# One run of small matmuls for the values of a pair of tiles and the scores of the next pair

## The chip, the cores and the metric

The kernel runs on one core of a Trainium2 chip (trn2). The metric is the device time of one execution in microseconds (us); lower is better. Engines are named as in the profile: PE (TensorE matmul), PEld (its weight loads), DVE (VectorE), ACT (ScalarE), POOL (GpSimd), SP (SyncE, which issues the DMAs).

## The reference

Three stages in a row, all in float32: chunked attention over 4 batches, 8 heads, 768 positions of width 64, and then two feed-forward layers (512 to 2048 to 512) over the 3072 tokens.

```python
for c in range(nc):                                  # chunks of 32 queries
    k_ctx = k[:, :, max(0, c*32 - 16) : min(S, c*32 + 40)]   # and v_ctx
    k_full = concatenate([mem_k, k_ctx], axis=2)     # 8 memory keys; v_full alike
    scores = q_c @ k_full.T / sqrt(64)
    a = exp(scores - max(scores)); a = a / (sum(a) + 1e-9)
    out[c] = a @ v_full
h = x @ w_in;  y = (max(h, 0) + alpha * min(h, 0)) @ moe_w_out      # layer 1
h = y @ w2_in; out = (h * tanh(softplus(h))) @ moe2_w_out           # layer 2
```

## The kernel before

The 3072 tokens are 24 tiles of 128 tokens and six blocks of four tiles. The attention of a block is computed while the layer 1 of the block before it runs; layer 2 follows after all of layer 1. Matrices of the layers are split into a high and a low part, so each product takes three matmuls.

**Layer 1.** For every block `blk` and every `j` of the 16 slices of the hidden width, `gemm1` (L990) does 12 large matmuls (128 x 512) into one PSUM bank, bank 4 or 5 by `j % 2`. `act1` (L1019) empties that bank with two activations on ACT (L1021, L1022), joins them on DVE (L1025) and splits the result into `gh` on ACT (L1015) and `gl` on DVE (L1016). `gemm2` (L1059, matmuls L1051) does 12 large matmuls into the accumulators in banks 0 to 3. A list `pend` keeps `gemm2` behind: with `LAG = 2` the order on PE is `gemm1(j)`, `gemm2(j-2)`, `gemm1(j+1)`, `gemm2(j-1)`, and so on.

**Attention.** From tile 4 on, tiles are taken in pairs `T`, `T+1`. `scores_late` (L699) does 128 small matmuls (64 rows, 32 columns of the array, 64 moving columns) into banks 6 and 7; then come maxima on DVE, 32 exponentials on ACT with their sums, and the normalisation on DVE. From tile 8 on (`UPT`) `turn_late` (L846) turns the result on DVE with 16 stream transposes (L877) into the one buffer `aT`. `values_late` (L776) does 128 small matmuls (64 rows, 64 columns, 32 moving columns), also into banks 6 and 7, which ACT (L810) and DVE (L813) empty into the `x` of the block. Each of these runs is one task of PE, a `burst` (L891): nothing comes between its matmuls.

**Order.** `block_steps` (L928) lists for every pair the steps `("s", T)`, None, a turn or None, `("v", T)`; `weave(p)` (L1355) spreads the eight steps of two pairs over 30 positions, two to each `j`: one after `gemm1(j)`, one after `gemm2(j-2)`. So a pair's scores and its values are two separate bursts among the large matmuls.

**The plan.** All tasks go into `Plan` (L68): each has an engine, an assumed duration, and what it reads and writes. PE's tasks get their place in the order in which they are added; every other task gets a due time counted back from the PE task that needs it, and each engine takes of its ready tasks the one that is due first. What comes out is a fixed order for each engine; on the chip each engine waits in that order.

**Loads of attention.** SP's queue loads `q` of a tile into `q_own[T % 2]`, and the keys of an even tile into `kring` (one buffer), its values into `vring` (one buffer). An odd tile has one room, `upper`, the upper halves of two buffers: its keys are loaded there (L522), and, when the scores have read them, its values (L559), into the same place.

**Weights of layer 1.** The second matrix has 16 slices in slots `("o", 0)` to `("o", 15)`. After the first block the slices from `AWAY = 10` on give their slots to other uses: each was stored to DRAM once (L1329) and is loaded again in every later block by `reload1` (L396, L400), through three slots in turn. Slots 13 to 15 serve the conversion of the layer 2 weights, which runs on ACT, DVE and SP during blocks 1 to 4.

## Time and profile before

| | |
|---|---|
| time, median of 3 runs | 1084.5 us (1083.97 to 1085.22) |
| the profiled execution: its time | 1084.67 us |
| its span, first to last instruction | 1082.9 us |
| PE busy | 1073.2 us, 99% of the span, 9299 matmuls |
| DVE, ACT busy | 729.5 us (67%), 657.0 us (61%) |
| DMA | 252.63 MB, mean 233 GB/s |

Matmuls overlap in the array, so the busy time of PE is not the sum of what single matmuls cost: that is read from the distance between starts. A row of the timeline merges neighbours of one kind: its start, the time from the start of the first to the end of the last, and the count. Idle time of an engine other than the one that sets the end costs nothing.

### The profile page before, as it was taken

What the parts mean: (1) busy time and instruction counts of PE and PEld (TensorE: products, weight loads), DVE (VectorE), ACT (ScalarE), POOL (GpSimd) and SP (SyncE); (2) the same over time, 40 slices, a digit from 0 to 9 for tenths busy, and PEclk for the clock granted to TensorE, in tenths of its full rate; (3) what the DMA queues carried; (4) which work ended last, traced back from release to release, by engine and by line L of the source; (5) the groups of instructions that cost most, each with busy time, mean ns of one, the idle gap of its engine ahead of it and who ended that gap; (6) DMA issues with size and microseconds to landing.
All of it is one profiled execution on the core that took longest, in us unless ns stands there. A gap on an engine that the chain in (4) does not pass through costs nothing.

```text
span 1082.9 us, 24507 instructions
## 1 busy us (share of the span) xinstructions
PE 1073.2 (99%) x9299; PEld 966.5 (89%) x9299; DVE 729.5 (67%) x1614; ACT 657.0 (61%) x1676; POOL 6.6 (1%) x19
## 2 busy tenths in 40 slices
PE   9999999999999999999999999999999999999997
PEld 6888888878888888888888999999999999999997
DVE  6899487677769768686322855676685676676555
ACT  6888456455464646555334766676676666666664
POOL 2000000000000000000000000000000000000000
PEclk9999999999999999999999999999999999999999
DMA  9957754775476577547764777887887888887875
GB/s 300 321 184 240 249 187 167 243 242 194 166 259 216 176 240 262 184 144 248 228 193 141 253 241 252 267 266 249 271 264 252 272 260 258 264 263 236 263 248 170
DMA packets 139942, 252.63 MB, mean 233 GB/s; under 512 B 13872, under 2 KB 45104, under 8 KB 139824
## 3 DMA queue, kind: packets, MB, share of 16 engines
q1 hardware_dynamic: 139824, 251.07, 72.1%
q8 instruction: 73, 1.20, 0.5%
q14 instruction: 45, 0.37, 0.1%
HBM read 205.92 MB, written 45.09 MB: 232 GB/s over the span
## 4 chain that ended last, share of the span: by engine, by line
PE 98%; DMA 1%; DVE 0%; ACT 0%; SPq 0%; issue 0%; DVEq 0%; ACTq 0%
PE bank L1003 24%; PE bank L1051 24%; PE bank L1183 22%; PE bank L1256 22%; PE bank L789 2%; PE bank L723 1%; PE bank L1313 1%; DMA raw<-in_w_in_dram 1%; PE bank L600 0%; PE bank L667 0%; PE bank L836 0%; SPq L559 0%; DVE rstrip L1277 0%; PE bank L860 0%; DVE e L1277 0%
## 5 line engine op out<-in xcount | busy, mean ns | idle before, releaser
L1003 PE MATMUL bank<-xh,wi 128*128 128x512 f32 (+1 forms) x784 | 254.8, 387 | 0.0
L1051 PE MATMUL bank<-gh,wo 128*128 128x512 f32 x768 | 253.9, 391 | 0.7 <-ACT rstrip L250 0.7
L1003 PEld LDWEIGHTS bank<-xh,wi 128*128 128x128 f32 x784 | 146.3, 188 | 30.0
L1051 PEld LDWEIGHTS bank<-gh,wo 128*128 128x128 f32 x768 | 144.2, 188 | 31.3 <-ACT rstrip L250 1.1
L1191 ACT COPY v<-bank 128x512 f32<-128x512 f32 x192 | 102.5, 534 | 114.4 <-PE bank L1183 111.4
L1003 PE MATMUL bank<-xl,wi 128*128 128x512 f32 (+1 forms) x392 | 150.9, 385 | 0.0
L1051 PE MATMUL bank<-gl,wo 128*128 128x512 f32 x384 | 149.5, 389 | 0.0
L1025 DVE SCALAR_TENSOR_TENSOR rstrip<-rstrip,nalpha 128x512 f32<-128x512 f32 x96 | 71.8, 748 | 70.9 <-ACT rstrip L1022 70.1
L1015 ACT CAST gh<-rstrip 128x512 fp32r<-128x512 f32 x96 | 60.2, 627 | 88.2 <-DVE rstrip L1025 47.9
L1021 ACT ACTIVATE rstrip<-bank 128x512 f32<-128x512 f32 x96 | 58.0, 604 | 87.6 <-PE bank L1003 85.2
L1194 DVE TENSOR_TENSOR v<-v,v 128x256 f32<-128x256 f32 x192 | 80.4, 423 | 44.2 <-ACT v L1191 42.7
L1016 DVE TENSOR_TENSOR gl<-rstrip,gh 128x512 fp32r<-128x512 f32 x96 | 66.3, 691 | 57.2 <-ACT gh L1015 56.8
L1197 ACT ACTIVATE v<-v 128x256 f32<-128x256 f32 x192 | 80.1, 418 | 36.7 <-DVE v L1194 34.2
L1194 DVE TENSOR_TENSOR v<-v 128x256 f32<-128x256 f32 x144 | 60.8, 423 | 51.9 <-ACT v L1191 48.1
L1003 PEld LDWEIGHTS bank<-xl,wi 128*128 128x128 f32 x392 | 73.7, 188 | 14.4
L1051 PEld LDWEIGHTS bank<-gl,wo 128*128 128x128 f32 x384 | 72.1, 188 | 14.6
L1183 PE MATMUL bank<-wo,wi 128*128 128x256 f32 x432 | 61.9, 283 | 0.6 <-ACT v L1191 0.6
L742 ACT ACTIVATE s<-bank,su 128x64 f32<-128x64 f32 x160 | 48.5, 350 | 19.7 <-DVE su L759 19.7
L877 DVE STREAM_TRANSPOSE aT<-s 32x256 f32<-32x256 f32 x128 | 55.7, 435 | 2.9
L1022 ACT ACTIVATE rstrip<-bank 128x512 f32<-128x512 f32 x96 | 57.5, 599 | 0.0
L1183 PEld LDWEIGHTS bank<-wo,wi 128*128 128x128 f32 x432 | 56.3, 192 | 1.1 <-ACT v L1191 1.0
L1183 PE MATMUL bank<-xl,wi 128*128 128x256 f32 x396 | 54.4, 283 | 0.0
(197 smaller groups left out, 1890.1 us busy)
## 6 DMA issues: line engine op xcount, KB each, us to landing
wi<-w2o SPq DMA_DIRECT2D x204, 256.0 KB, 3.5
wo<-w2o SPq DMA_DIRECT2D x132, 256.0 KB, 3.4
wo<-w1o SPq DMA_DIRECT2D x30, 512.0 KB, 4.5
w2o<-wo SPq DMA_DIRECT2D x56, 256.0 KB, 2.4
wi<-w2s SPq DMA_DIRECT2D x56, 256.0 KB, 3.5
wo<-in_w_out_dram SPq DMA_DIRECT2D x24, 512.0 KB, 7.7
w2k<-wo SPq DMA_DIRECT2D x40, 256.0 KB, 2.2
wo<-w2s SPq DMA_DIRECT2D x40, 256.0 KB, 3.3
```

The source lines that it names most:

```text
L1003: nc.tensor.matmul(bk.t[:, lo:hi], a, b, start=kk == 0 and i == 0, stop=kk == KT - 1 and i == 2)
L1015: add("act", a_(n), lambda: nc.scalar.copy(g.t[0], src.t[0]), [src], [(g, "h")])
L1016: add("dve", d_(n), lambda: nc.vector.tensor_sub(g.t[1], src.t[0], g.t[0].bitcast(F32)), [src, (g, "h")], [(g, "l")])
L1021: add("act", a_(n) - 0.05, lambda: nc.scalar.activation(m.t[0], h.t[:, :n], AF.Relu, scale=-1.0), [h], [m])
L1022: add("act", a_(n) - 0.05, lambda: nc.scalar.activation(r.t[0], h.t[:, :n], AF.Relu), [h], [r])
L1025: lambda: nc.vector.scalar_tensor_tensor(r.t[0], m.t[0], nalpha[:, j : j + 1], r.t[0], ALU.mult, ALU.add),
L1051: nc.tensor.matmul(bk.t[:, :n], lt, rh, start=j == 0 and i == 0, stop=j == NJ - 1 and i == 2)
L1183: nc.tensor.matmul(X.t[:, half * HB : (half + 1) * HB], l, r, start=start and kk == n == 0, stop=kk == 1 and n == 2, skip_group_check=True,)
L1191: add("act", c_(n * HB), lambda: nc.scalar.copy(e.t[:, : n * HB], X.t[:, : n * HB]), [X], [(e, i) for i in range(n)])
L1194: add("dve", e_(HB), lambda: op(at(to), at(a), at(b)), [v[a], v[b]], [v[to]])
L1197: add("act", c_(HB), lambda: nc.scalar.activation(at(name), at(name), AF.Mish), [], [v[name]])
L1256: nc.tensor.matmul(bk.t[:, s * HB : (s + 1) * HB], g.t[:, zg * HB + s * P : zg * HB + (s + 1) * P], piece()[:, zw * HB : (zw + 1) * HB], s ...
```

## The change

From tile 8 on, the values of pair `T` and the scores of pair `T+2` become one burst of kind `"vs"`. There are seven of these (`T` = 8 to 20 in steps of two); the scores of pair 8 and the values of pair 22 stay alone, as do both bursts of pairs 4 and 6.

The values of a joint burst go into the two banks of `gemm1`, `4 + (j+1) % 2` and `4 + j % 2`, and the scores into banks 6 and 7, so that it writes four banks. It is put only at an odd position, after `gemm2(j-2)`, and behind it `ahead()` brings the oldest pending `gemm2`, that of `j-1`, forward. The order on PE is then `gemm1(j)`, `gemm2(j-2)`, burst, `gemm2(j-1)`, `gemm1(j+1)`, `gemm1(j+2)`, `gemm2(j)`.

When the burst is issued, the values of an odd tile and the keys of the next odd tile must both be there. So odd tiles get a second room in slot `("o", 12)`, and the two rooms are taken in turn by pairs. `AWAY` falls from 10 to 9: slices 9 to 15 are stored and loaded again, through slots 9 to 11. All loads for the next pair follow the burst.

```diff
@@ -281,7 +281,8 @@
     w2s = dp.tile([P, NPAIR * len(SENT), 512], F32, name="w2s")
     w2o = dp.tile([P, NPAIR * 7, 512], F32, name="w2o")
     w2_bufs = {"k": Buf(None), "s": Buf(None), "o": Buf(None)}
-    AWAY = 10
+    AWAY = 9
+    ROOM = 12
     w1o = dp.tile([P, NJ - AWAY, 1024], F32, name="w1o")
     w1o_buf = Buf(None)
 
@@ -507,6 +508,17 @@
         kts[T], qs[T] = (kt, kview), (qt, qview)
         att_bufs.append(kt)
 
+    rooms = [upper]
+
+    def room(T):
+        return rooms[T // 2 % 2 if T >= UPT else 0]
+
+    def open_room():
+        before = slots["o", ROOM]
+        b = slot("o", ROOM, [P, 1024], F32)
+        rooms.append([Buf(lambda lo=lo: b.t[:, lo : lo + 512], before) for lo in (0, 512)])
+        slots["o", ROOM] = rooms[1]
+
     def load_qk_late(T):
         b, t = divmod(T, TPB)
         qt = q_own[T % 2]
@@ -515,8 +527,8 @@
             lambda: nc.sync.dma_start(qt.t, q[b, t].rearrange("h d a e x -> (h d) (a e x)")), writes=[qt],
         )
         if T % 2:
-            bufs = upper
-            for i, u in enumerate(upper):
+            bufs = room(T)
+            for i, u in enumerate(bufs):
 
                 def part(i=i, u=u):
                     nc.sync.dma_start(
@@ -548,12 +560,12 @@
             att_bufs.append(v)
             return
 
-        bufs = upper if T % 2 else [vring.next()]
+        bufs = room(T) if T % 2 else [vring.next()]
         for e in range(2):
             half = slice(e * 64, (e + 1) * 64)
             rows = vw[b, 2 * t + e].rearrange("w h d -> w (h d)")
             if T % 2:
-                for c, u in enumerate(upper):
+                for c, u in enumerate(bufs):
 
                     def part(c=c, u=u, half=half, rows=rows):
                         nc.sync.dma_start(u.t[half], rows[c * CH : c * CH + SW])
@@ -773,10 +785,10 @@
 
         return go, [b for i in range(2) for b in kts[T + i][0] + qs[T + i][0]], bks, rest
 
-    def values_late(T):
+    def values_late(T, places=(6, 7)):
         ab, aT = aTs.pop(T)
         vs = [vws.pop(T + i) for i in range(2)]
-        bks = [bank(6), bank(7)]
+        bks = [bank(i) for i in places]
 
         def go():
             for i, (_, value) in enumerate(vs):
@@ -891,14 +903,23 @@
     def burst(T, kind, *parts):
 
         add(
-            "pe", 1.15 if T < T0 else {"s": 1.55, "v": 2.1}[kind], lambda: [go() for go, _, _, _ in parts],
-            sum((r for _, r, _, _ in parts), behind(T)), sum((w for _, _, w, _ in parts), []),
+            "pe", 1.15 if T < T0 else {"s": 1.55, "v": 2.1, "vs": 3.35}[kind], lambda: [go() for go, _, _, _ in parts],
+            sum((r for _, r, _, _ in parts), behind(T) if kind != "vs" else []), sum((w for _, _, w, _ in parts), []),
         )
         for *_, rest in parts:
             rest()
 
-    def run_step(st):
+    def run_step(st, free=None):
         kind, T = st
+        if kind == "vs":
+            burst(T, kind, values_late(T, free), scores_late(T + 2))
+            load_v(T + 3)
+            load_v(T + 2)
+            for T2 in (T + 4, T + 5):
+                if T2 < NTT:
+                    load_qk(T2)
+            turn_late(T + 2)
+            return
         if kind == "t":
             (turn_pe if T < T0 else turn_late)(T)
         elif kind == "v":
@@ -912,7 +933,7 @@
             T2 = T + 1 if T < T0 else T + 2
             if T2 < NTT:
                 load_qk(T2)
-                if T < T0:
+                if T < T0 or T >= UPT:
                     load_qk(T2 + 1)
         if kind == "v" and T >= T0 - 1:
             T2 = T + 1 if T < T0 else T + 2
@@ -928,7 +949,10 @@
     for blk in range(1, NBA):
         steps = []
         for T in range(blk * TB, (blk + 1) * TB, 2):
-            steps += [("s", T), None, ("t", T) if T < UPT else None, ("v", T)]
+            if T < UPT:
+                steps += [("s", T), None, ("t", T), ("v", T)]
+            else:
+                steps += [("s", T) if T == UPT else None, None, None, ("vs", T) if T + 2 < NTT else ("v", T)]
         block_steps.append(steps)
 
 
@@ -1341,6 +1365,8 @@
     LAG = 2
     tiles = [(0, blk, j) for blk in range(NBA) for j in range(NJ)]
     pend = []
+    joint = []
+    open_room()
     xcur = xts[0]
     xnext = None
     n_in = 0
@@ -1352,10 +1378,22 @@
         att = block_steps[blk + 1] if layer == 0 and blk + 1 < NBA else []
         p0 = P0 if blk == 0 else 0
 
+        def ahead():
+            done = pend.pop(0)
+            if done[1] and done[2] >= AWAY:
+                reload1(done[2])
+            gemm2(*done)
+
         def weave(p):
             lo, hi = ((len(att) * max(x - p0, 0) + NPOS - p0 - 1) // (NPOS - p0) for x in (p, p + 1))
             for st in filter(None, att[lo:hi]):
-                run_step(st)
+                if st[0] == "vs":
+                    joint.append(st)
+                else:
+                    run_step(st)
+            if joint and p % 2:
+                run_step(joint.pop(), (4 + (j + 1) % 2, 4 + j % 2))
+                ahead()
 
         if j == 0:
             if blk == NBA - 1:
@@ -1373,10 +1411,7 @@
         act1(blk, j, h, n)
         pend.append((layer, blk, j))
         while len(pend) > LAG:
-            done = pend.pop(0)
-            if done[1] and done[2] >= AWAY:
-                reload1(done[2])
-            gemm2(*done)
+            ahead()
         if blk == NBA - 1:
             while n_in < len(in_places) and in_places[n_in][0] <= j:
                 reload_in(n_in)
```

## Rows read from the trace of the kernel before

**Rows 1.** Page: granted clock in 40 slices, and the chain that ended last.

```profile
PEclk9999999999999999999999999999999999999999
...
PE 98%; DMA 1%; DVE 0%; ACT 0%; SPq 0%; issue 0%; DVEq 0%; ACTq 0%
```

**Rows 2.** Waits of PE from 20 us on: line, releaser, us, times, longest.

```profile
PE bank L1051 <- ACT rstrip L250: 0.7, 1, 0.7
PE bank L1183 <- ACT v L1191: 0.6, 1, 0.6
```

**Rows 3.** Instructions of L723 and of L789: count, duration ns, first and last start.

```profile
L723 PE MATMUL bank<-kt,qbd x640: 212/216/243, 37.8 to 451.9; 64*32 64x64 f32 x160
...
L789 PE MATMUL bank<-aT,vw x640: 219/219/241, 64.9 to 483.8; 64*64 64x32 f32 x160
```

**Rows 4.** Chain in order of time: one undisturbed group of 12 large matmuls.

```profile
47.69 2.72 PE bank L1051 x12
```

**Rows 5.** Timeline of PE around the values of pair 8: start, us, line, count.

```profile
152.15 0.39 PE L1051 MATMUL bank<-gh,wo 128*128 128x512 f32 x1
152.47 1.14 PE L789 MATMUL bank<-aT,vw 64*64 64x32 f32 x64
153.42 1.11 PE L789 MATMUL bank<-aT,qbd 64*64 64x32 f32 x64
154.47 0.50 PE L1003 MATMUL bank<-xh,wi 128*128 128x512 f32 x1
...
157.32 0.39 PE L1051 MATMUL bank<-gh,wo 128*128 128x512 f32 x1
```

**Rows 6.** Timeline of PE around the scores of pair 10.

```profile
165.26 0.39 PE L1051 MATMUL bank<-gh,wo 128*128 128x512 f32 x1
165.58 0.86 PE L723 MATMUL bank<-kt,qbd 64*32 64x64 f32 x64
...
166.74 0.34 PE L723 MATMUL bank<-qbd 64*32 64x64 f32 x12
167.02 0.49 PE L1003 MATMUL bank<-xh,wi 128*128 128x512 f32 x1
...
169.88 0.39 PE L1051 MATMUL bank<-gh,wo 128*128 128x512 f32 x1
```

**Rows 7.** Timeline of PE in the first attention: four small runs behind each other.

```profile
13.23 0.92 PE L836 MATMUL bank<-ident,s 64*96 64x64 f32 x16
14.07 1.19 PE L600 MATMUL bank<-wo,wi 128*64 128x64 f32 x32
15.10 1.10 PE L667 MATMUL bank<-aT,vw 96*64 96x64 f32 x32
16.13 0.92 PE L836 MATMUL bank<-ident,wo 64*96 64x64 f32 x16
```

**Rows 8.** Windows: length, busy times of the engines, granted clock, DMA.

```profile
13.20:17.00 3.80, 3.80 (x97) 3.56 (x97) 2.49 (x7) 3.47 (x20) 0.00 (x0) 1.00 1.09 308
```

**Rows 9.** Timeline of PE in the scores of pair 16.

```profile
311.57 0.86 PE L723 MATMUL bank<-kt,qbd 64*32 64x64 f32 x64
...
312.36 0.32 PE L723 MATMUL bank<-qbd,qbd 64*32 64x64 f32 x13
```

**Rows 10.** Timeline of all engines ahead of and behind the values of pair 12.

```profile
245.28 0.39 PE L1003 MATMUL bank<-xh,wi 128*128 128x512 f32 x1
...
247.07 0.62 ACT L1015 CAST gh<-rstrip 128x512 fp32r<-128x512 f32 x1 [5.66 <-DVE rstrip L1025]
...
248.09 0.59 ACT L1022 ACTIVATE rstrip<-bank 128x512 f32<-128x512 f32 x1
248.32 1.02 PEld L789 LDWEIGHTS bank<-aT,vw 64*64 64x64 f32 x64 [0.35 <-issue]
...
251.88 0.69 DVE L813 TENSOR_TENSOR xl<-bank,xh 128x512 fp32r<-128x512 f32 x1
```

**Rows 11.** Reloads of L400: from issue to landing, min/median/max.

```profile
DMA to landing us min/median/max: 3.7/4.5/6.6
```

## The prediction

> **What bounds the kernel now.** I read the page first: the chain that ended last lies to 98% on PE, and the granted clock is full in all 40 slices [rows 1], so the end moves only when PE does less or waits more. The waits of PE come next: from 20 us on there are two, of 0.7 and 0.6 us, and neither is near an attention burst [rows 2]. There is no wait for this change to remove. What is left is time inside PE's own stream, and for that the timeline has to be read by starts, because matmuls overlap (a small one lasts 0.22 us, but its neighbour starts long before that) [rows 3].

> The undisturbed stream is 12 large matmuls in 2.72 us, 0.227 us each [rows 4]. Around the values of pair 8 the stream shows this [rows 5]:

> - In: the last large matmul starts at 152.15, so the next thing could start at 152.377. The first small one starts at 152.47: 0.093 us lost.
> - The run itself: the last of the 128 starts at 153.42 + 1.11 - 0.219 = 154.311 and its pitch is (1.11 - 0.219) / 63 = 0.014, so the run is over at 154.325, after 1.855 us.
> - Out: the next large matmul starts at 154.47: 0.145 us lost. Its group of 12 takes until 157.32, 2.85 us and not 2.72: 0.13 us more.

> The values are a detour of 2.22 us, of which 0.37 us is switching. The scores are the same picture [rows 6]: in 165.58 - 165.487 = 0.093, the run 1.294 us at a pitch of 0.0102, out 167.02 - 166.874 = 0.146, and a first group of 2.86 us, 0.14 over; together 1.67 us. Each line has 640 matmuls of its first half, 64 to a burst, so there are ten bursts of each kind [rows 3].

> **The change part by part.** *The joint burst.* Seven times, the way out of the values (0.145 + 0.13) and the way into the scores (0.093) go: 0.368 us. In their place comes a switch from values (64 x 64 of the array) to scores (64 x 32), which the trace of before does not hold. The nearest rows are the four small runs behind each other in the first attention [rows 7]. With 0.22 us as length of one matmul, L836 has a pitch of 0.70 / 15 = 0.047, is over at 13.977, and L600 starts at 14.07: 0.09 us. L600 (128 x 64) to L667 (96 x 64), in the same way, 15.10 - 15.071 = 0.03. L667 to L836 (64 x 96), 16.13 - 16.008 = 0.12. The two rows in which the columns change cost 0.09 and 0.12, the one in which they stay 0.03. Here the columns change, so I take 0.10; the bounds are 0 (no switch at all) and 0.368 (as dear as the way through the large matmuls). That is 0.268 us a burst, 7 x 0.268 = 1.88 us.

> [...]

> *Length of the burst.* It becomes some 3.5 us of small matmuls. The granted clock stays 1.00 through 3.8 us of small runs with nothing large between them [rows 8], so I cost that at nothing.

> *Banks of the values.* The values now wait for the two activations of `act1(j)` on ACT; the group `gemm2(j-2)`, 2.72 us, hides them where ACT is prompt. Everything on PE is queued behind that wait. The other side: `gemm1(j+1)` needs the first of the two banks back. In the trace the first subtraction behind the values of pair 12 ends at 251.88 + 0.69 = 252.57 [rows 10], 2.25 us after that run (248.32 + 2.00, the length as in [rows 5]); between lie now the scores (1.29), the way out (0.15) and `gemm2(j-1)` (2.86), 4.3 us. Nothing, with 2 us to spare; without that cover, 2.25 us a burst.

> *`ahead`.* `gemm2(j-1)` moves before `gemm1(j+1)`, but behind the burst, so its `g` has more time than before (3.5 us against 2.72). The work on PE is the same.

> *Loads.* After a joint burst SP's queue gets the loads that came in two portions: values of an odd tile 4 x 128 KB, of an even tile 2 x 256 KB, `q` 2 x 256 KB, keys 336 and 2 x 168 KB, 2.2 MB, some 9 us at the mean 233 GB/s. The next joint burst is 15 positions of 2.72 us, 41 us, later: nothing. What stands behind them in the queue are the reloads of layer 1 (35 instead of 30) and the layer 2 conversion. A reload lands in 4.5 us, 6.6 at most [rows 11]; its slot comes free three `gemm2` ahead, 3 x 5.44 less the 2.72 by which `ahead` brings one forward, 13.6 us: hidden; one that is late would cost PE up to 6.6 us. The one store more lies with the six others behind the first block's loads; PE does not wait for it.

> **The sum.** The profiled execution took 1084.67 us, 0.17 above the median of the runs and well within their spread of 1.25. 1084.67 - 1.88 = 1082.8; from the median it would be 1082.6. I predict 1082.7 us. That is 0.17% less, and 0.2% (2.2 us) is about what a measurement of this kernel tells from no change.

> **The rivals.**

> *No drain in the middle, so faster.* For it: 64 rows stay 64 rows, and the row with equal columns cost 0.03 [rows 7]. Against it: here the columns do change. With 0.03 the gain is 7 x 0.338 = 2.37, 1082.3 us; with 0, 1082.1. It passes 0.2% from a switch of 0.058 us down.

> *The joint run is not what it says, so no gain.* Either the middle switch costs all of 0.368, or the longer stream of small matmuls has holes. The scores of pair 16 have one: their second half should start at 311.57 + 64 x 0.0102 = 312.22 and starts at 312.36, and nothing in the profile released it [rows 9]. Against it: of the bursts on which this rests it is one; the pitch of [rows 6] runs through. Two such holes in each joint burst cost 7 x 0.28 = 1.96 us: 1084.7 us.

> *ACT is late for the values' bank, so slower.* ACT works in a fixed order. Ahead of the values of pair 12 it stood 5.66 us for DVE before a cast, with the two activations behind that; `gemm1`'s last matmul had started at 245.28, and the second activation ended at 248.09 + 0.59 = 248.68, 0.36 us after the values started [rows 10]. Before, that was harmless: the values took banks 6 and 7. Now PE would stand some 0.4 us. From 0.27 us a burst the gain is gone, and from (1.88 + 2.17) / 7 = 0.58 the kernel is slower by 0.2%. The worst that row allows: had the matmuls ended when ACT began to stand, the activations would end 5.66 + (248.68 - 247.07) = 7.3 us later, a wait of over 4 us, 7 x 4 = 28 us. With 0.4 in each burst the time is 1085.6, with 1 us, which I take as its middle, 1084.67 - 1.88 + 7 = 1089.8. Against it: the plan now counts these activations due before the values and will take them ahead of exponentials; and a pair has 15 or 16 positions instead of 11 from scores to values, 41 us instead of 30, so DVE's turning is done earlier and does not pile up there.

> **How the numbers follow.** Forecast, a middle switch of 0.06 to 0.12 and at most two or three short waits: 0.45, 1082.4 to 1083.7. No drain: 0.25. No gain: 0.18. ACT late by enough to be slower: 0.12. The range holds the first three, from 1082.1 less the half spread of the runs (0.6), 1081.5, up to the lighter end of the last, 1085.6; I leave out the heavier part of it, some 0.1, and a little below. Faster by over 0.2% is the second case and the lower edge of the forecast (0.07): 0.32. Slower is the last: 0.12. Within 0.2%: 0.56.

> **What would show it.** In the timeline of PE after: nine entries into small matmuls from tile 8 on instead of sixteen; a joint run of 1.86 + 0.10 + 1.29 us, with one group of 2.86 behind it; the gap between last value and first score is the disputed number. Right on ACT: no wait of PE for L1021, L1022, L810 or L813. Wrong would be the prediction if PE's waits name these lines seven times, or if it waits for a reload (L400) or an odd tile's loads (L522, L559).

## The result, and the profile after

The changed kernel takes 1098.42 us (four runs, 1097.1 to 1099.61) against 1084.24 us: ratio 1.0129, 95% interval 1.0117 to 1.014. It is 14.2 us slower, outside the predicted range. The span of the profiled execution grew from 1082.9 to 1096.8 us.

The page of the changed kernel, of which the first line and the chain answer to [rows 1] (L735 is now the line of the scores, L801 of the values, L1027 of `gemm1`, L1075 of `gemm2`):

```profile
span 1096.8 us, 24496 instructions
...
q8 instruction: 73, 1.20, 0.5%
...
PE 98%; issue 1%; DVE 0%; ACT 0%; DVEq 0%; ACTq 0%
```

A share of the chain has grown from 0% to 1%: "issue", time in which PE waited for nothing that the profile names. The waits of PE say where, beside [rows 2]: line, releaser, us, times, longest.

```profile
PE bank L735 <- issue: 11.2, 7, 2.6
...
PE bank L735 <- PE bank L801: 0.5, 1, 0.5
```

Seven times for seven joint runs, in the scores. No line of ACT, DVE or a load (L822, L825, L1045, L534, L571) is among PE's releasers in attention. The timeline of PE in the first joint run, values of pair 8 with scores of pair 10, which answers to [rows 5] and [rows 6]:

```profile
152.16 0.39 PE L1075 MATMUL bank<-gh,wo 128*128 128x512 f32 x1
152.48 1.14 PE L801 MATMUL bank<-aT,vw 64*64 64x32 f32 x64
153.44 1.11 PE L801 MATMUL bank<-aT,qbd 64*64 64x32 f32 x64
154.48 0.80 PE L735 MATMUL bank<-kt,qbd 64*32 64x64 f32 x60
...
156.44 0.83 PE L735 MATMUL bank<-wo,qbd 64*32 64x64 f32 x60 [1.06 <-issue]
157.19 0.50 PE L1075 MATMUL bank<-gh,wo 128*128 128x512 f32 x1
...
160.05 0.39 PE L1027 MATMUL bank<-xh,wi 128*128 128x512 f32 x1
```

The values end at 153.44 + 1.11 - 0.219 + 0.014 = 154.345 and the scores start at 154.48: the disputed switch costs 0.135 us. Then, with 68 of 128 scores issued, PE stands still. What happened meanwhile is in the DMA view of two stretches, 154.1 to 155.2 and 155.2 to 156.5; the first holds one packet, the second none of that queue.

```profile
DMA packets 1, 0.02 MB, mean 15 GB/s; under 512 B 0, under 2 KB 0, under 8 KB 0
...
q8 instruction: 1, 0.02, 5.6%
```

```profile
DMA packets 15, 0.04 MB, mean 31 GB/s; under 512 B 0, under 2 KB 0, under 8 KB 15
...
q1 hardware_dynamic: 15, 0.04, 14.4%
```

Queue q8 carries 73 packets of 16 KB in all. The trace holds 18,834 instructions of PE, which is 73 packets of 256 and a rest of 146; 64 bytes an instruction is my estimate from these two counts. I took the start and length of each packet from the trace and counted where in PE's program (weight loads, matmuls, semaphore waits) the first matmul behind each hole stands, modulo 256 (its place within a block of 256):

```
joint run  hole from, to (us)   place mod 256   last q8 packet, end   from its end to resuming
152.48     155.16  156.44       197             154.12, 155.10        1.33
200.94     202.79  203.55       197             201.06, 202.06        1.49
200.94     204.83  207.11       196             204.66, 205.82        1.30
252.61     255.20  256.82       197             254.23, 255.38        1.44
301.42     304.63  307.41       197             304.98, 305.97        1.44
351.45     353.98  355.43       196             353.00, 353.97        1.46
400.12     403.29  405.59       197             403.19, 404.14        1.45
451.24     453.68  454.65       196             452.41, 453.37        1.28
```

All eight holes lie at one place of a period of 256, wherever that falls in the run, and each ends 1.28 to 1.49 us after a packet of instructions has landed. The one from 202.79 to 203.55, between values and scores, is the wait that the view puts down to L801. (Counted from the records of the trace alone, the places are 193 and 194; what matters is that they agree.) The reading is that PE has run out of instructions; the experiments test it.

A second cost follows in two runs. The timeline of PE behind the run at 200.94:

```profile
207.11 0.21 PE L735 MATMUL bank<-qbd 64*32 64x64 f32 x1 [2.06 <-issue]
207.25 0.50 PE L1075 MATMUL bank<-gh,wo 128*128 128x512 f32 x1
207.59 0.56 PE L1075 MATMUL bank<-gl,wo 128*128 128x512 f32 x1
207.95 1.05 PE L1075 MATMUL bank<-gh,wo 128*128 128x512 f32 x2
...
211.70 0.40 PE L1027 MATMUL bank<-xh,wi 128*128 128x512 f32 x1
```

The large matmuls start 0.43 us apart instead of 0.227, and the group takes 211.70 - 207.25 = 4.45 us instead of 2.86. The windows view of that stretch (length, busy times, granted clock, DMA) shows half the clock, 0.51:

```profile
207.60:211.00 3.40, 3.40 (x10) 2.63 (x9) 3.40 (x7) 0.41 (x1) 0.00 (x0) 0.51 0.09 34
```

**The account.** Measured as in the prediction, from the last large matmul before to the end of the group behind, the first joint run costs 157.19 + 0.14 - 152.387 = 4.94 us; the seven are 4.94, 8.13, 5.29, 6.50, 5.15, 7.59 and 4.68, together 42.3 us. The fourteen runs that they replace cost 27.5. That is 14.8 us, and the span grew by 13.9; the 0.7 us wait of L1051 in [rows 2] is gone. Nearly all of it is the holes: less the ordinary distance between starts, the eight are 13.2 us, and the large matmuls at half clock add 1.6 us and 1.3 us; the switches saved give 1.6 us back.

### The profile page after: what moved, and what is told of

Read it like the earlier page. It is cut to its first block, busy times and chain, and to the rows that moved or that the text cites. A ratio compares the mean times of both kernels' runs of the same rounds, so it can differ in the third digit from the quotient of the medians.

```text
span 1096.8 us, 24496 instructions
## 1 busy us (share of the span) xinstructions
PE 1076.0 (98%) x9299; PEld 969.9 (88%) x9299; DVE 725.6 (66%) x1610; ACT 657.6 (60%) x1680; POOL 6.6 (1%) x19
## 4 chain that ended last, share of the span: by engine, by line
PE 98%; issue 1%; DVE 0%; ACT 0%; DVEq 0%; ACTq 0%
PE bank L1075 24%; PE bank L1027 24%; PE bank L1207 22%; PE bank L1280 22%; PE bank L801 2%; PE bank L735 1%; PE bank L1337 1%; PE bank L612 0%; PE bank L679 0%; PE bank L848 0%; DVE rstrip L1301 0%; PE bank L872 0%; DVE e L1301 0%; ACT L1221 0%; DVEq L1497 0%
## 5 line engine op out<-in xcount | busy, mean ns | idle before, releaser
L1075 PE MATMUL bank<-gh,wo 128*128 128x512 f32 x768 | 256.0, 394 | 0.0
L1027 PE MATMUL bank<-xh,wi 128*128 128x512 f32 (+1 forms) x784 | 252.7, 386 | 0.0
L1075 PEld LDWEIGHTS bank<-gh,wo 128*128 128x128 f32 x768 | 145.6, 190 | 33.3 <-DMA kt<-in_kw_dram 2.5
L1027 PEld LDWEIGHTS bank<-xh,wi 128*128 128x128 f32 x784 | 146.3, 188 | 29.6
L1027 PE MATMUL bank<-xl,wi 128*128 128x512 f32 (+1 forms) x392 | 150.8, 385 | 0.0
L1075 PE MATMUL bank<-gl,wo 128*128 128x512 f32 x384 | 150.6, 392 | 0.0
L1045 ACT ACTIVATE rstrip<-bank 128x512 f32<-128x512 f32 x96 | 58.1, 606 | 92.6 <-PE bank L1027 92.4
L1027 PEld LDWEIGHTS bank<-xl,wi 128*128 128x128 f32 x392 | 73.7, 188 | 14.6
L1075 PEld LDWEIGHTS bank<-gl,wo 128*128 128x128 f32 x384 | 72.8, 190 | 14.8
L371 ACT CAST wo<-wo 128x256 fp32r<-128x256 f32 x64 | 24.1, 406 | 52.3 <-DVE wo L365 47.8
```

What stands on the lines that cost most here:

```text
L1027: nc.tensor.matmul(bk.t[:, lo:hi], a, b, start=kk == 0 and i == 0, stop=kk == KT - 1 and i == 2)
L1045: add("act", a_(n) - 0.05, lambda: nc.scalar.activation(m.t[0], h.t[:, :n], AF.Relu, scale=-1.0), [h], [m])
L1075: nc.tensor.matmul(bk.t[:, :n], lt, rh, start=j == 0 and i == 0, stop=j == NJ - 1 and i == 2)
```

## The experiments

The theory ("supply theory" below): PE's instructions arrive in blocks of 256, and only the next block is ahead. While large matmuls run, 256 instructions take 29 us (128 x 0.227); in a joint run they take 1.3 to 1.9 us, and in the eight cases of the table the next block was there 2.6 to 4.3 us after the one before it had been entered. A run of 128 small matmuls with their weight loads, 256 instructions, gets by (no wait at L723 or L789 in [rows 2]); a joint run, 512, cannot. The rivals: the room, the banks and the loads; or a limit on runs of small matmuls as such.

**Large matmuls between the two parts.** In three kernels all else of the change stays (the edit, shortened):

```diff
-            burst(T, kind, values_late(T, free), scores_late(T + 2))
+            burst(T, "vv", values_late(T, free))
+            between()       # 12, 6 or 3 of the matmuls of gemm2(j-1); the rest follow the scores
+            burst(T, "ss", scores_late(T + 2))
```

> All parts of the change stay (second room, three reload slots from slice 9 on, values in the banks of gemm1, the order of the loads), but gemm2(j-1) stands between the values and the scores, so no run of small matmuls holds more than 128. Supply theory (PE runs out of instructions: they come in blocks of 256, one block ahead, and a joint run of 128 + 128 small matmuls with their weight loads is 512 instructions): no hole in any run, switching as before, 1084.2 us, between 1083.5 and 1085.5. Rival (the room, the banks, the reloads or the order of the loads cost time by themselves): holes or waits stay in or around the scores, 1090 us or more.

> The same with six large matmuls between. Supply theory: 1.6 us and 15 instructions more between the boundaries; no hole in six of the joint runs, 0.3 to 0.8 us twice in the one that begins 4 instructions before a boundary: 1084.3 to 1086 us. Rival (length of the run as such): 1084.3 us.

> The changed kernel with three of the twelve matmuls of gemm2(j-1) between the values and the scores of a joint run, the other nine behind it. Supply theory: from one boundary of 256 instructions to the next there must be some 2.9 to 3.3 us; the three large matmuls and the switch add 0.9 us and 8 instructions to the 1.9 us of before, so holes shrink from 1.1 to 2.8 us to 0 to 0.8 us each, in all 1 to 5 us: 1085 to 1089 us. Rival (a run of small matmuls fails as such, above a length between 128 and 256): no run is longer than 128 now, no hole at all, 1084.3 us.

With twelve: 1083.91 us, ratio 0.9995 (0.9986 to 1.0004), as expected. The room, the banks, the reloads and the order of the loads cost nothing that the time shows. With six 1087.88, with three 1096.04 (one run each; single runs of the kernel before reach 1087.09, so for six the three holes count and not the time). The waits of PE in scores, first with six, then with three:

```profile
PE bank L735 <- issue: 3.4, 3, 1.6
```

```profile
PE bank L735 <- issue: 7.6, 7, 3.3
```

With twelve there is none. All holes are at the block boundary again, and all ten end 1.24 to 1.70 us after a packet. Three large matmuls still leave seven holes though no run is longer than 128, so the length of a run as such is out. Both times are above what I expected, six by 2 and three by 7 us: with six, three runs had holes where I counted on one. Those three came to the second boundary 2.5 to 3.0 us after the first, the other four 3.2 to 3.4 us after it, with a delay of at most 0.13 us. But the block can take longer than the 2.9 to 3.3 us that I counted on: in the run at 392.64 the first boundary is crossed at 394.31, the packet starts only at 396.14, and PE resumes at 399.03, 4.7 us after the crossing. With three, one hole of 3.3 us and 6.8 us at half clock behind it carry much of the excess.

**The values twice, in the kernel before.** The plan's assumed duration of these runs goes from 2.1 to 4.0 us with it.

```diff
-            for i, (_, value) in enumerate(vs):
+            for i, (_, value) in list(enumerate(vs)) * (2 if T >= UPT else 1):
```

> The kernel before, with the values of the pairs from tile 8 on computed twice in the same run (the same results written again), so eight runs of 256 small matmuls, with nothing of the change: no second room, old banks, old loads. The second computation costs 8 x 1.86 = 14.9 us of PE. Supply theory: where both block boundaries fall well inside the run (counted in the program, in five of the eight: after 138, 126, 113, 100 and 247 of its 512 instructions) a hole of 1.2 to 1.6 us at the second boundary, where the first is crossed at the start (30, 17, 4) little or none; in all 5 to 12 us of holes, 1104 to 1111 us, 1106.7 us. Rival (holes come from the new room, banks or loads): no hole, 1099.2 us.

1118.05 us (one run), with nothing of the change in it. Holes: in the five runs expected, and behind two of the others, in the first large matmuls. The waits:

```profile
PE bank L789 <- issue: 7.1, 5, 1.9
PE bank L1051 <- DVE xl L813: 1.8, 1, 1.8
...
PE bank L1051 <- issue: 0.8, 1, 0.8
```

The rival's 1099.2 fails. The time is 7 us above my upper bound. The seven holes are 11.6 us between starts, at the upper end of what I expected; I had not counted that the clock fell to half in four stretches, 17 us in all. The wait of 1.8 us that the view puts down to DVE is the hole behind the run at 406.69: it lies at a block boundary and ends 1.44 us after a packet.

**Moving the boundaries.** Empty instructions (padding of the program to an address, in PE's stream; what they cost, the control below measures) are spread among the large matmuls ahead of each joint run, so that every run begins the same distance before a boundary. The work and its order stay (the edit, shortened):

```diff
             def go(kk=kk, views=views, k0=k0, at=pads_of(blk, j, -1)):
+                if at:      # (8, 0) in 40 to 48 groups of three matmuls ahead of a run,
+                    nc.tensor.addr_align(at[0], offset=at[1])   # (256, offset) in the last one
                 xh, xl = (t[:, kk - k0, lo:hi] for t in views())
```

> The changed kernel, with some 840 empty instructions spread among the large matmuls, so that each of the seven joint runs begins 14 instructions before a boundary of 256. Nothing else differs. Supply theory: the first boundary is crossed ahead of the run, while the sequencer still runs ahead of large matmuls, the second has its block by then, the third comes some 7 large matmuls after the run: holes of 0 to 0.4 us a run instead of 1.1 to 2.8, and 7 x 0.23 = 1.6 us of saved switching: 1082.6 us, between 1082 and 1086. Rival (data, banks, or the length of the run of small matmuls as such): holes as in the changed kernel, 1097 to 1100 us.

> The same with each joint run beginning 240 instructions before a boundary, some 870 empty instructions. Supply theory: one hole of 2.0 to 2.9 us in every one of the seven runs, at instruction 496 of 512, that is 8 matmuls before the end of the scores, where the changed kernel had this place in two runs only: 1098 to 1110 us, 1101 us. Rival: as in the changed kernel, holes at different places of the runs, 1098.4 us.

> The kernel before with as many empty instructions (854) in the same places among the large matmuls as the aligned kernels have. Supply theory as far as it holds for the aligned kernels needs them to be free: 1084.3 us, within 0.1%. Rival: each costs PE time, 20 ns or more, 1101 us or more, and the times of the aligned kernels say nothing about the holes.

At 240 instructions ahead: 1119.27 us (one run); each of the seven runs has a hole of 1.9 to 4.0 us between starts, behind matmul 246 or 247 of 256, within two of the place counted beforehand; five have a first one of 0.4 to 1.0 us behind matmul 119, where the first boundary lies, which I had not expected. The waits of PE in scores and values, and the timeline of PE at the end of the run at 362.76:

```profile
PE bank L735 <- issue: 16.3, 7, 3.8
PE bank L801 <- issue: 2.7, 5, 0.8
```

```profile
365.42 0.74 PE L735 MATMUL bank<-wo,qbd 64*32 64x64 f32 x53
367.86 0.32 PE L735 MATMUL bank<-wo,qbd 64*32 64x64 f32 x9 [1.69 <-issue]
```

All seven are followed by half clock, 3.4 to 6.8 us each. I had counted neither that nor the first holes, and the time is 9 us above my upper bound. Moving nothing but the boundary moved the holes; the data, the banks and the loads are those of the changed kernel.

At 14 ahead: 1098.21 us, ratio 1.0135 (1.0116 to 1.0154). The holes moved as they should, but did not vanish; my 1082.6 was wrong. The timeline of PE in the run at 203.12:

```profile
205.12 0.31 PE L735 MATMUL bank<-kt,qbd 64*32 64x64 f32 x6
205.81 0.81 PE L735 MATMUL bank<-kt,qbd 64*32 64x64 f32 x58 [0.38 <-issue]
...
207.21 0.50 PE L1093 MATMUL bank<-gh,wo 128*128 128x512 f32 x1
207.54 0.39 PE L1093 MATMUL bank<-gl,wo 128*128 128x512 f32 x1
207.78 0.40 PE L1093 MATMUL bank<-gh,wo 128*128 128x512 f32 x1
209.15 0.50 PE L1093 MATMUL bank<-gh,wo 128*128 128x512 f32 x1 [0.98 <-issue]
```

The second boundary (270 instructions in, score 7) is crossed at 205.81; the next packet runs from 206.91 to 207.84 and PE resumes at 209.15, 3.3 us after the crossing. To the third boundary PE needs only some 2 us: 242 instructions of scores, three large matmuls, and empty instructions, which stand again among the large matmuls right behind the run. I had counted seven large matmuls to there. In the last run, which has no empty instructions behind it, six came before the boundary, and the hole was still 2.44 us. And in four of seven runs the second boundary was late too, because the first had not been crossed ahead: their packets start after the run has begun, those of the other three before. (Among the large matmuls of the changed kernel, the four packets from 521 to 607 us start some 0.7 to 4.2 us before PE reaches the boundary, by the count of its records.)

The control, the kernel before with 854 of these instructions: 1085.81 us, ratio 1.0012 (1.0002 to 1.0023). Close to free, by 0.12% not quite, so they do not account for the 14 and 35 us of the aligned kernels.

**Half the instructions, the same joint run.** The edit, shortened:

```diff
-                                    out[h * 64 : (h + 1) * 64, i, p, c],
-                                    value(half, c, 2 * p + h),
-                                    aT()[half, i, ...
+                                    out[h * 64 : (h + 1) * 64, 0:2, p, c],
+                                    value(half, c, 2 * p + h),          # of the first tile alone
+                                    aT()[half, 0:2, ...                 # scores alike
```

> The changed kernel with joint runs of half the instructions: in them each small matmul streams twice the columns and fills the places of both tiles, so that the second tile's scores come from the first tile's queries and keys and its values from the first tile's value rows (the output is not the reference's for those tiles). Banks, rooms, loads, four banks in one run and the direct switch from values to scores stay; a joint run is 256 instructions. Supply theory: no hole in any joint run; the run lasts between 1.8 us (same pitch) and 3.5 us (same columns a second), so 1070.5 to 1083 us. Rival (two kinds of small matmuls in one run, four banks, or the loads): holes of 1 us and more stay.

1073.16 us (one run), and from 20 us on PE has no wait in attention. The timeline of PE in its first joint run:

```profile
151.84 1.16 PE L801 MATMUL bank<-aT,vw 64*64 64x64 f32 x64
152.93 1.16 PE L735 MATMUL bank<-kt,qbd 64*32 64x128 f32 x64
```

Two kinds in one run, four banks, the second room and the loads are all there, and with 256 instructions there is no hole as before in any of the seven. Six cost 2.43 us with their switches. The one at 197.79 costs 2.59: it begins at a block boundary, reaches the next one at its end, and starts the large matmul behind it 0.39 us after its last small one instead of 0.20, 1.35 us after a packet. So in this kernel 256 instructions in 2.2 us are at the edge of what the supply gives. The halved run is also shorter, 2.2 us instead of 3.5, and by itself does not part the count of instructions from the length; the moved boundaries do.

No version here that computes the whole attention beats the kernel before: what the joint run saves needs 512 instructions in 3.5 us.

## Why the prediction was wrong

- *The step that failed* is "Length of the burst", costed at nothing: I asked of the longer run only whether the clock holds, and cited 3.8 us of small runs in the first attention. That stretch holds 97 matmuls [rows 8]; a joint run holds 256 in 3.5 us. The thing to compare was instructions a microsecond, not the length. What the term cost in the runs is 13.2 us of holes and 2.9 us of half clock behind them. The rival with holes named the place, but was priced from the one small hole of [rows 9], 0.14 us twice a run, 1.96 us, and given 0.18. The holes last 0.8 to 2.8 us between starts. Shown by the boundaries that move them and by the halved run, whose one delay is 0.19 us. What caused the 0.14 us of [rows 9] stays open: by the same count it lies within three instructions behind a block boundary, but the last packet before it had ended at 299.44, 12.8 us earlier, so a late block does not explain it.
- *The switch in the middle* was right in kind: 0.135 us against the 0.10 taken from [rows 7]. Seven times (0.368 - 0.135) is 1.6 us saved, not 1.88. It is really there, as far as the arithmetic of the runs tells; no kernel with full work shows it as a time. Whether the array drains at that switch, as the first rival's name has it, no run shows.
- *ACT late for the values' bank* (the rival on the slow side, 0.12): did not occur. PE waits neither for the activations nor for the copies out of the banks. The direction was this rival's, the mechanism was not.
- *Banks, `ahead`, loads, reloads at nothing*: right, and shown, by the kernel with twelve large matmuls between (0.9995).
- *The clock*: "I cost that at nothing" held for the small matmuls themselves (the granted clock is 1.00 from 152.40 to 155.20, up to the hole of the first joint run), and failed for what the holes did: two stretches at half clock cost 4.45 - 2.86 = 1.6 us in the first and 4.20 - 2.86 = 1.3 in the second.

What the prediction needed stands in the DMA view of before:

```profile
q8 instruction: 73, 1.20, 0.5%
```

## What to carry to other kernels

Count instructions, not only matmuls and microseconds, when small matmuls are put together: in this kernel a stretch of 512 PE instructions in 3.5 us starves, one of 256 gets by, and a group of twelve large matmuls between two such stretches feeds it again (six do not always). "Issue" in the waits of an engine that hardly waits otherwise (11.2 us in seven waits), at places a fixed number of instructions apart (256), was the sign here; the profile's queue of kind "instruction" shows the packet that lands 1.28 to 1.49 us before PE goes on. Where small matmuls must be many, the lever here was fewer and wider ones (1073.16 us), not their grouping (1098.42); that is shown for the time alone, because the halved run does not compute the full attention.

## What was not expected of the hardware

- A small matmul of twice the columns cost far less than twice: 64 of the values took 1.16 us with 64 columns and 1.14 with 32 [rows 5]; 64 of the scores took 1.16 us with 128 columns and 0.86 with 64 [rows 6].
- A hole among the small matmuls can be followed by half clock (granted 0.51 in the changed kernel, 0.50 in the one aligned at 240) for 3.4 or 6.8 us. This was so behind two of the changed kernel's seven runs (2.3 us between starts), behind four of the five holes among small matmuls in the kernel with the values twice (1.5 to 2.2), behind one of the seven with three large matmuls between (3.5), and behind all seven runs with a boundary close to their end. It was not so behind the hole of 2.78 us between starts in the run at 301.42, nor behind any of the eleven in the kernel aligned at 14, four among small and seven among large matmuls. What decides is open.
- From crossing a boundary to having the block after it took PE 2.6 to 4.3 us in the changed kernel and up to 5.5 in the others. The packet itself is 0.9 to 1.5 of it, and the time from its landing to the first instruction 1.2 to 1.7. The rest passes before the packet starts, 0.1 to 1.8 us in the changed kernel; why that differs is open.
